# Unequal half blocks in a gated FFN after windowed attention: five pairs of 512, 512, 512, 384, 384 tokens instead of four pairs of 464 and one of 448

## The chip, the cores and the metric

The kernel runs on one core of a Trainium2 chip. The metric is the device time of one execution in microseconds (us). Beside each time there is a profile of one execution: its span, from the first to the last instruction, and what each engine did. The engines are PE (TensorE; PEld is its weight load), DVE (VectorE), ACT (ScalarE), POOL (GpSimd) and SP (SyncE, which here issues all the DMAs).

## The reference

Causal attention with a window of 128 positions and a linear bias over 8 batches, 8 heads, 576 positions, 64 per head; its output, 4608 tokens of 512, goes through a gated FFN of width 1536:

```python
scores = q @ k.T / 8 - slope[h] * |i - j|, kept where 0 <= i - j < 128
x = (softmax(scores) @ v) -> [4608, 512]
gate = 1 / (1 + exp(-(x @ w_gate)))          # w_gate, w_val: [512, 1536]
out = (gate * (x @ w_val)) @ w_out           # w_out: [1536, 512]
```

Weights arrive as 8-byte floats and are decoded on the chip to 4-byte ones.

## The kernel before

Every product of the FFN is done in three passes: both operands are split into a high and a low part (`parts`: a cast, then a subtraction), and high x high, high x low and low x high are summed in PSUM.

The work has three stages.

1. Attention, together with the first four of the twelve 128-wide chunks of the FFN's hidden layer h (`gates1`, line 514). It takes the tokens in nine tiles of 512; each output chunk of a tile is 12 matmuls of 512 columns (line 534).
2. The other eight chunks (`gates2`, line 586). The 4608 tokens are taken in five pairs of half blocks; `HALVES[t]` is the length N of a half block in pair t, and `EDGE` holds where each starts. Gate and value weights and the two half blocks are combined in a scheme of seven products for eight (Strassen's, in Winograd's form). `mix` makes the seven combinations of x for the pair (`combo`, the tiles cxA, cxB, cxC, each high and low part); `combine` made those of the weights once (w2s0 to w2s5, and w2s6 and w2s7 in the tile `w67`). A chunk is seven products of 6 matmuls of N columns each (line 616), 42 in all.
3. The output projection (`results`, line 683), in the same scheme and over the same five pairs. h has been written to DRAM (`hs`) by `spill` and is read back in four quadrants (half block h, half k of the hidden layer), each in three pieces of two chunks (`hquad`). For each of seven products and each third e the combination of h is split into one of `NHC` places (`hcombo`), and 12 matmuls of N columns follow (line 728), so a pair has 7 x 36 = 252 matmuls.

Stages 2 and 3 together have 5 x (8 x 42 + 252) = 2940 matmuls, 588 for each pair, whatever N is.

The ring (`ring`, line 200) is one tile of NRING places of N2 = max(HALVES) columns. Stage 1 uses its first 2048 columns as four places of 512. In stage 2 a chunk takes three places in turn (`scratch`): for a partial sum that is only read back, and for two results that are spilled to `hs`. In stage 3 a pair takes eight: two each for `a1`, `p5`, `u2` and `x`, which are stored to the output.

Where the quadrants of h lie: (0,0) in the place of xr, the input of `mix`; the other three in `hr`, in the place of `w67` (tag wA). The h pieces have nine places: seven are the combos of x, the two more (`hw`) lie in the weights' scratch (tag xW), which `combine` uses while it prepares the weights of the output projection (`wos`, in the places of w2s0 to w2s5).

The order of instructions on each engine is fixed beforehand by a planner (`Graph.order`): it lists every operation with an estimated cost, and each time starts the one that can start first. PE's order is thus fixed too: an operand that comes later than planned makes PE wait. `follow` says that a buffer's new contents must wait until its old ones were used. The planner's cost of a PE group is, for six matmuls,

```python
g.add("PE", 6 * (N / 2400 + 0.0133), six, ...
```

The last call of `gates2` takes the chunks in the order 6, 7, 0, 1, 2, 3, 4, 5, since `hr` waits for w2s6 and w2s7, and `wos{c}` for w2s{c}.

Of the kernel before, what the change touches and what calls it, by code (L numbers as in the profile page):

```python
# [8 lines left out]
F32 = mybir.dt.float32  # L9
I32 = mybir.dt.int32  # L10
F32R = mybir.dt.float32r
# [4 lines left out]
P = 128  # L16
# [7 lines left out]
NFC = DFF // P  # L24
NB = 512
NTB = NT // NB
FC1 = 4
GRP = 2
HALVES = (464, 464, 464, 464, 448)
N2, NT2 = max(HALVES), len(HALVES)  # L30
EDGE = [2 * sum(HALVES[:b // 2]) + b % 2 * HALVES[b // 2] for b in range(2 * NT2)] + [NT]
HC = NFC // 6
NRING, NRING1, NHC = 10, 4, 9
HEAD = 8
RUN = 4
NPB, NST, NPT, NBOTH = 8, 10, 3, 3
# [11 lines left out]
NRAW = 2  # L48
# [110 lines left out]
def attention_gated_ffn(ctx: ExitStack, tc: tile.TileContext, qd, kd, vd, wg, wv, wo, out):  # L159
# [6 lines left out]
    moe = ctx.enter_context(tc.tile_pool(name="moe", bufs=1))  # L166
# [6 lines left out]
    def T(pool, name, shape, dtype, tag=None):  # L173
        if name not in made:
            made[name] = pool.tile(shape, dtype, tag=tag or name, name=name)
        return made[name]
# [50 lines left out]
    xs = [dram.tile([KC, P, S], F32, name=f"xs{b}") for b in range(B)]  # L227
    hs = [[dram.tile([NFC // 2, P, HALVES[b // 2]], F32, name=f"hs{k}_{b}") for b in range(2 * NT2)] for k in range(2)]
    wod = [dram.tile([P, DM], F32, name=f"wod{f}") for f in range(NFC)]
# [20 lines left out]

    w1 = lambda kind, part_: T(moe, "w1", [P, 2, 2, FC1, DM], F32R, tag="wA")[:, "gv".index(kind), part_]
    w67 = lambda: T(moe, "w67", [P, 2, 2, 7, 2 * P], F32R, tag="wA")
    hr = lambda: T(moe, "hr", [P, 3, NFC // 2, N2], F32, tag="wA")
    w2t = lambda i, part_: w67()[:, i - 6, part_] if i > 5 else T(pools["w2"], f"w2s{i}", [P, 2, 7, 2 * P], F32R, tag=f"W{i}")[:, part_]
    wot = lambda c, part_: T(pools["w2"], f"wos{c}", [P, 2, 7, 2 * P], F32R, tag=f"W{c}")[:, part_]
    x1 = lambda part_: T(moe, "x1", [P, 9 * DM], F32R, tag="xB")[:, part_ * KC * NB:(part_ + 1) * KC * NB].rearrange("p (c t) -> p c t", c=KC)
# [1 line left out]
    wraw = lambda s: work()[:, s * 2 * DM:(s + 1) * 2 * DM].rearrange("p (f t) -> p f t", t=2)  # L258
    wbits = lambda s: work()[:, (4 + s) * DM:(5 + s) * DM]
# [298 lines left out]
    ORDER = (0, 3, 4, 1, 5, 2, 6)  # L558
# [7 lines left out]
    def combo(k, part_):  # L566
        j, grp = [(j, n) for n, ks in (("xA", (0, 3, 4)), ("xB", (1, 5, 2)), ("xC", (6,))) for j, kk in enumerate(ks) if kk == k][0]
        return T(moe if grp == "xB" else pools["w2"], f"c{grp}", [P, 1 if grp == "xC" else 3, 2, 2, N2], F32R, tag=grp)[:, j, part_]
# [17 lines left out]
    def gates2(t, chunks, f0):  # L586
        F = FIRST + 1
        N, t0 = HALVES[t], EDGE[2 * t]
        xr = lambda: xrow()
# [83 lines left out]
        split(6, x(1, 1), xk[1, 1])  # L673

    hq0 = lambda: T(moe, "hq0", [P, NFC // 2, N2], F32, tag="xr")
    hquad = lambda h, k: hq0() if h == k == 0 else hr()[:, {(1, 0): 0, (1, 1): 1, (0, 1): 2}[h, k]]

    def hcombo(s, part_):
        if s < len(ORDER):
            return combo(ORDER[s], part_)  # L680
        return T(moe, "hw", [P, 2, 2, HC, N2], F32R, tag="xW")[:, s - len(ORDER), part_]

    def results(t):
        F, N, t0 = FIRST + 2, HALVES[t], EDGE[2 * t]
        third = [slice(e * HC, (e + 1) * HC) for e in range(3)]
# [8 lines left out]
        def split(k, e, val, reads):  # L694
            s = slots[k, e]
            parts(lambda: hcombo(s, 0)[:, :, 0:N], lambda: hcombo(s, 1)[:, :, 0:N], val, m, reads, ("hc", s, 0), ("hc", s, 1), F)
# [10 lines left out]
        def product(k, banks_, start):  # L707
            for e in range(3):
                v = lambda a, b, e=e: (lambda: hquad(a, b)[:, third[e], 0:N])
                q = lambda a, b: hk[a, b, e]  # L710
                if k == 3:
                    add(v(1, 0), v(1, 0), v(1, 1), ALU.add, q(1, 1), q(1, 0))
                elif k == 4:
                    add(v(1, 0), v(1, 0), v(0, 0), ALU.subtract, q(0, 0), q(1, 0))
                elif k == 5:
                    add(v(0, 1), v(0, 1), v(1, 0), ALU.subtract, q(1, 0), q(0, 1))
                    add(v(1, 0), v(1, 1), v(1, 0), ALU.subtract, q(1, 1), q(1, 0))
                a, b = {0: (0, 0), 3: (1, 0), 4: (1, 0), 1: (0, 1), 5: (1, 0), 2: (0, 1), 6: (1, 1)}[k]
                split(k, e, v(a, b), q(a, b))
                s = slots[k, e]  # L720
                for i in range(2):
                    if len(banks_) == i:
                        banks_.append(bank())

                    def six(i=i, e=e, s=s):
                        for c in range(HC):
                            for j, (xp, wp) in enumerate(((0, 0), (0, 1), (1, 0))):
                                nc.tensor.matmul(mm[banks_[i]][:, 0:N], wot(e * HC + c, wp)[:, k, i * P:(i + 1) * P], hcombo(s, xp)[:, c, 0:N],  # L728
                                                 start=(start and e == c == j == 0), stop=(e == 2 and c == HC - 1 and j == 2),
                                                 skip_group_check=True)  # L730
                    wa = 0 if k < 1 else 1
                    g.add("PE", 3 * HC * (N / 2400 + 0.0133), six,
                          [("hc", s, 0), ("hc", s, 1)] + [("wo", e * HC + c, p, wa) for c in range(HC) for p in range(2)],
                          [("mm", banks_[i])], 1.0e6)
# [74 lines left out]
    def follow(old, new):  # L809
        g.add("PY", 0.0, lambda: None, [], [*old, *new], FIRST)  # L810

    both_ = lambda *k: [(*k, p) for p in range(2)]
# [5 lines left out]
    w2k = lambda i: [("w2", i, p, a) for p in range(2) for a in (0, 2)]  # L818
# [17 lines left out]
        wsrc = [wo[f] for f in range(NFC)]  # L836
    for t in range(NT2 - 1):
        gates2(t, range(NW), FC1)
    gates2(NT2 - 1, (6, 7, 0, 1, 2, 3, 4, 5), FC1)
    follow(w2k(6) + w2k(7), [("hq", h, k, e) for h, k in ((1, 0), (1, 1), (0, 1)) for e in range(3)])  # L840
    follow([("xr", k, (h, e)) for k in range(2) for h in range(2) for e in range(2)], [("hq", 0, 0, e) for e in range(3)])
    follow([("wraw", s) for s in range(NRAW)], [("tt", 1)])
    for c in range(NFC // 2):
        follow(w2k(c), wok(c))
        combine(wsrc[c], wsrc[c + NFC // 2], 1, lambda p, c=c: wot(c, p), ("wo", c), [("wod", c), ("wod", c + NFC // 2)], FIRST + 1.5, c % 2)
    for s0, c in enumerate(ORDER):
        follow(both_("xc", c), both_("hc", s0))
    follow([("wraw", s) for s in range(NRAW)] + [("wbits", s) for s in range(2)] + [("tt", j) for j in range(2)], both_("hc", 7) + both_("hc", 8))
    for t in range(NT2):
        results(t)  # L850
    g.play()
# [51 lines left out]
```

## Time and profile before

| | |
|---|---|
| median of three runs | 1022.43 us (1020.39 to 1022.81) |
| profiled execution, its time | 1021.79 us |
| its span | 1020.1 us |
| PE busy | 1002.2 us (98%), 6450 matmuls |
| PEld busy | 848.3 us (83%) |
| DVE, ACT, POOL busy | 786.0, 499.1, 116.9 us |
| DMA | 158.48 MB, mean 155 GB/s |
| mean granted PE clock | 0.996 |
| first matmul of stage 2 | at 400.6 us |
| last matmul's end | at 1015.6 us |

A row of the timeline or the windows counts instructions in flight in its stretch. The mean duration of a matmul is its latency; matmuls are pipelined, so what a matmul takes of the time is the distance from its start to the next one's start, which is shorter.

### The profile page before, as it was taken

Reading aid. Unit: us, or ns where it says so; the run is one execution under the profiler, and the core shown is the slowest. Engines: PE = TensorE matmul, PEld = TensorE weight load, DVE = VectorE, ACT = ScalarE, POOL = GpSimd, SP = SyncE. Lnnn points to the kernel's source line nnn. Section 1 sums busy time; section 2 is a strip of 40 time slices with the busy share of each in tenths; the row PEclk is TensorE's granted clock in tenths of the full one; section 3 lists DMA queues with packets and bytes.
Section 4 is the critical chain, followed back from the end, with each engine's and each line's share of the span. In section 5 each row is a group of like instructions: output and inputs, shape, how many; then the busy total and the mean of one; then the engine's idle time right before and its main releaser. Section 6 shows DMA issues by size and latency. Waiting matters only on the chain.

```text
span 1020.1 us, 18313 instructions
## 1 busy us (share of the span) xinstructions
PE 1002.2 (98%) x6450; PEld 848.3 (83%) x6450; DVE 786.0 (77%) x2011; ACT 499.1 (49%) x1309; POOL 116.9 (11%) x214
## 2 busy tenths in 40 slices
PE   9899899999999999999999999999999999999998
PEld 7667677777777788888888888889988888888897
DVE  7999888888868897869447356365898888898881
ACT  6998777777864334445334334343464423222220
POOL 2333343333320000100000000000100000000000
PEclk9999899999999999999999999999999999999999
DMA  8776765656435554774313113116435363534201
GB/s 288 262 235 205 228 213 196 231 162 232 145 116 186 168 184 157 241 240 156 130 47 122 57 56 129 57 57 245 144 106 199 114 186 114 170 128 137 100 3 70
DMA packets 88316, 158.48 MB, mean 155 GB/s; under 512 B 11680, under 2 KB 63776, under 8 KB 88224
## 3 DMA queue, kind: packets, MB, share of 16 engines
q1 hardware_dynamic: 88224, 157.32, 46.1%
q8 instruction: 50, 0.82, 0.3%
q14 instruction: 42, 0.34, 0.1%
HBM read 106.95 MB, written 50.33 MB: 154 GB/s over the span
## 4 chain that ended last, share of the span: by engine, by line
PE 75%; DVE 13%; ACT 7%; issue 2%; DMA 2%; SPq 0%; DVEq 0%; ACTq 0%
PE mm L616 34%; PE mm L728 26%; PE mm L534 11%; ACT pb L391 4%; DVE mm L376 3%; DVE pb L388 2%; DVE pb L412 1%; PE mm L416 1%; PE mm L477 1%; ACT pb L411 1%; PE mm L353 1%; DVE st L406 1%; DVE x L189 1%; DMA work<-in_moe_w_gate_dram 1%; PE mm L363 1%
## 5 line engine op out<-in xcount | busy, mean ns | idle before, releaser
L534 PE MATMUL mm<-x,w 128*128 128x512 f32 x864 | 222.5, 402 | 3.7 <-DVE x L189 2.6
L534 PEld LDWEIGHTS mm<-x,w 128*128 128x128 f32 x864 | 155.2, 188 | 44.2 <-issue 7.6
L391 ACT ACTIVATE pb<-pb,st 128x128 f32<-128x128 f32 x288 | 112.8, 395 | 39.8 <-DVE st L388 39.4
L427 POOL TENSOR_SCALAR_AFFINE_SELECT pt<-both 128x384 f32<-128x384 f32 x192 | 100.4, 546 | 193.0 <-ACT both L180 163.6
L616 PE MATMUL mm<-cxB,w2s 128*128 128x464 f32 (+1 forms) x540 | 119.5, 372 | 0.1
L616 PE MATMUL mm<-cxA,w2s 128*128 128x464 f32 (+1 forms) x540 | 118.5, 370 | 0.0
L728 PE MATMUL mm<-cxA,wos 128*128 128x464 f32 (+1 forms) x540 | 114.4, 370 | 0.0
L616 PEld LDWEIGHTS mm<-cxB,w2s 128*128 128x128 f32 x540 | 101.5, 188 | 12.2 <-ACT ring L180 0.5
L623 DVE TENSOR_TENSOR mm<-mm,ring 128x464 f32<-128x464 f32 (+1 forms) x80 | 51.3, 643 | 77.9 <-PE mm L616 77.8
L728 PEld LDWEIGHTS mm<-cxA,wos 128*128 128x128 f32 x540 | 101.3, 188 | 11.1
L616 PEld LDWEIGHTS mm<-cxA,w2s 128*128 128x128 f32 x540 | 101.3, 188 | 11.0
L627 ACT ACTIVATE sg<-mm 128x464 f32<-128x464 f32 (+1 forms) x80 | 44.4, 556 | 120.7 <-PE mm L616 76.0
L180 ACT COPY ring<-mm 128x464 f32<-128x464 f32 (+1 forms) x119 | 64.6, 544 | 75.3 <-PE mm L616 74.9
L728 PE MATMUL mm<-cxB,wos 128*128 128x464 f32 (+1 forms) x360 | 77.2, 372 | 0.0
L728 PEld LDWEIGHTS mm<-cxB,wos 128*128 128x128 f32 x360 | 67.7, 188 | 7.8
L388 DVE CUSTOM_DVE_ANT_0 pb<-mm,relm 128x128 f32<-128x128 f32 x288 | 68.4, 284 | 1.7
L188 POOL TENSOR_TENSOR work<-work 128x256 f32<-128x256 f32 x9 | 11.7, 1304 | 431.7 <-DMA work<-wod 296.9
L416 PE MATMUL mm<-ident,pb 128*128 128x128 f32 x288 | 52.9, 289 | 7.5 <-ACT both L180 4.1
L740 ACT ACTIVATE ring<-mm 128x464 f32<-128x464 f32 (+1 forms) x40 | 22.2, 555 | 75.9 <-PE mm L728 75.9
L376 DVE COPY_PREDICATED mm<-swap,mm 64x128 f32<-64x128 int32 x216 | 55.2, 294 | 4.8 <-PE mm L363 1.2
L411 ACT ACTIVATE pb<-pb,st 128x128 f32<-128x128 f32 x157 | 54.1, 395 | 8.7 <-DVE st L408 8.5
L416 PEld LDWEIGHTS mm<-ident,pb 128*128 128x128 f32 x288 | 33.1, 142 | 27.9 <-ACT both L180 10.3
(107 smaller groups left out, 1620.5 us busy)
## 6 DMA issues: line engine op xcount, KB each, us to landing
kr<-in_k_dram SPq DMA_DIRECT2D x31, 576.0 KB, 4.7
hr<-hs SPq DMA_DIRECT2D x36, 464.0 KB, 4.6
hs<-ring SPq DMA_DIRECT2D x68, 232.0 KB, 2.0
qr<-in_q_dram SPq DMA_DIRECT2D x31, 320.0 KB, 5.1
vr<-in_v_dram SPq DMA_DIRECT2D x32, 288.0 KB, 3.7
xs<-xt SPq DMA_DIRECT2D x32, 288.0 KB, 3.1
out_dram<-ring SPq DMA_DIRECT2D x32, 232.0 KB, 2.5
work<-in_moe_w_gate_dram SPq DMA_DIRECT2D x12, 512.0 KB, 4.3
```

The source lines that it names most:

```text
L180: g.add("ACT", act_cost(n, psum), lambda: nc.scalar.copy(out(), src()), reads, writes, want, release=release, ways=[("DVE", dve_cost(n, ps ...
L376: g.add("DVE", dve_cost(2 * D, psum=True), lambda b=b, col=col, to=to, of=of: nc.vector.copy_predicated(sp[b][col, :, to:to + D], swap[col ...
L388: g.add("DVE", 0.21, lambda: nc.vector.tensor_tensor_reduce(pb()[:, e], sp[j // 2][:, j % 2, first:first + P], relm[u.p][:, w], op0=ALU.ad ...
L391: g.add("ACT", 0.39, lambda: nc.scalar.activation(pb()[:, e], pb()[:, e], AF.Exp, bias=st()[:, e:e + 1], scale=-1.0, accum_out=st()[:, 3 + ...
L411: g.add("ACT", 0.3, lambda args=args: nc.scalar.mul(*args()), [(kst, 6)], [(kpb, e)], want, ways=[("DVE", 0.16, True, lambda args=args: nc ...
L416: nc.tensor.transpose(tp[:, e], pb()[:, e], ident)
L427: nc.gpsimd.affine_select(pt(u)[:, f0:f0 + 2 * n - 1:2, :], both(), [[0, n], step], cmp, 0.0, base=0, channel_multiplier=mult)
L534: nc.tensor.matmul(mm[s], w1(kind, wi)[:, i, c * P:(c + 1) * P], x1(x)[:, c, :], start=(k == 0 and c == 0), stop=(k == 2 and c == KC - 1))
L616: nc.tensor.matmul(mm[b][:, 0:N], w2t(i, wp)[:, wk, c * P:(c + 1) * P], combo(k, xp)[:, c, 0:N], start=(start and c == 0 and j == 0), stop ...
L623: g.add("DVE", dve_cost(N, psum=True), lambda: nc.vector.tensor_tensor(o(), bk(b)(), a(), op=ALU.add), [("mm", b), *reads] if okeys else r ...
L627: g.add("ACT", act_cost(N, psum=True), lambda: nc.scalar.activation(sg[h](), bk(b)(), AF.Tanh, scale=0.5), [("mm", b)], [("sg", h)], F)
L728: nc.tensor.matmul(mm[banks_[i]][:, 0:N], wot(e * HC + c, wp)[:, k, i * P:(i + 1) * P], hcombo(s, xp)[:, c, 0:N], start=(start and e == c ...
```

## The change

The total number of tokens stays 4608 and the number of matmuls stays the same; three pairs have half blocks of 512 tokens, two of 384. N2 grows from 464 to 512, and with it each buffer that holds a half block. To make room, the ring has six places instead of ten, h pieces seven instead of nine, and `hr` two quadrants instead of three; the quadrant (0,1) of h goes into the weights' scratch, where the two extra h pieces were, and so waits until the last `combine` has been done. In the last call of `gates2` the order of chunks becomes 0, 6, 1, 7, 2, 3, 4, 5.

```diff
-HALVES = (464, 464, 464, 464, 448)
+HALVES = (512, 512, 512, 384, 384)
...
-NRING, NRING1, NHC = 10, 4, 9
+NRING, NRING1, NHC = 6, 4, 7
...
-    hr = lambda: T(moe, "hr", [P, 3, NFC // 2, N2], F32, tag="wA")
+    hr = lambda: T(moe, "hr", [P, 2, NFC // 2, N2], F32, tag="wA")
+    hw = lambda: T(moe, "hw", [P, NFC // 2, N2], F32, tag="xW")
...
-    hquad = lambda h, k: hq0() if h == k == 0 else hr()[:, {(1, 0): 0, (1, 1): 1, (0, 1): 2}[h, k]]
+    hquad = lambda h, k: hr()[:, k] if h else hw() if k else hq0()
 
     def hcombo(s, part_):
-        if s < len(ORDER):
-            return combo(ORDER[s], part_)
-        return T(moe, "hw", [P, 2, 2, HC, N2], F32R, tag="xW")[:, s - len(ORDER), part_]
+        return combo(ORDER[s], part_)
...
-    gates2(NT2 - 1, (6, 7, 0, 1, 2, 3, 4, 5), FC1)
-    follow(w2k(6) + w2k(7), [("hq", h, k, e) for h, k in ((1, 0), (1, 1), (0, 1)) for e in range(3)])
-    follow([("xr", k, (h, e)) for k in range(2) for h in range(2) for e in range(2)], [("hq", 0, 0, e) for e in range(3)])
+    gates2(NT2 - 1, (0, 6, 1, 7, 2, 3, 4, 5), FC1)
+    hq = lambda *hk: [("hq", h, k, e) for h, k in hk for e in range(3)]
+    follow(w2k(6) + w2k(7), hq((1, 0), (1, 1)))
+    follow([("xr", k, (h, e)) for k in range(2) for h in range(2) for e in range(2)], hq((0, 0)))
...
-    follow([("wraw", s) for s in range(NRAW)] + [("wbits", s) for s in range(2)] + [("tt", j) for j in range(2)], both_("hc", 7) + both_("hc", 8))
+    follow([("wraw", s) for s in range(NRAW)] + [("wbits", s) for s in range(2)] + [("tt", j) for j in range(2)], hq((0, 1)))
```

## The prediction

> **What bounds the kernel now.** I read the page's head first, then the chain of work that ended last, then the windows and the timeline of PE in the last two stages.
>
> ```profile
> span 1020.1 us, 18313 instructions
> PE 1002.2 (98%) x6450; PEld 848.3 (83%) x6450; DVE 786.0 (77%) x2011; ACT 499.1 (49%) x1309; POOL 116.9 (11%) x214
> PEclk9999899999999999999999999999999999999999
> ...
> 336.60 64.21 PE mm L534 x282
> 400.81 341.33 PE mm L616 x1632
> 749.50 1.49 PE mm L616 x6
> 751.00 2.52 PE mm L728 x12
> 753.52 1.22 PE mm L616 x6
> 754.74 260.84 PE mm L728 x1248
> ```
>
> From 336.60 us to the end the chain is PE alone, matmul behind matmul, at full granted clock. The windows of these stages:
>
> ```profile
> core 0: us, PE busy (x) PEld busy (x) DVE busy (x) ACT busy (x) POOL busy (x), PEclk, DMA share, GB/s
> 345.00:395.00 50.00, 50.00 (x223) 41.39 (x222) 41.85 (x71) 17.66 (x28) 0.00 (x0) 1.00 0.58 197
> 425.00:675.00 250.00, 250.00 (x1188) 222.71 (x1187) 143.87 (x216) 96.62 (x167) 3.10 (x3) 1.00 0.33 111
> 700.00:745.00 45.00, 45.00 (x225) 41.88 (x224) 35.03 (x56) 17.41 (x29) 5.40 (x5) 1.00 0.58 198
> 740.00:760.00 20.00, 19.89 (x97) 17.88 (x96) 19.34 (x27) 13.63 (x19) 1.95 (x2) 1.00 0.21 72
> 770.00:940.00 170.00, 170.00 (x808) 151.53 (x807) 146.58 (x158) 53.59 (x68) 0.00 (x0) 1.00 0.48 151
> 400.64:1015.56 614.92, 614.81 (x2941) 551.95 (x2939) 444.75 (x576) 225.09 (x347) 11.69 (x9) 1.00 0.38 125
> ```
>
> Stages 2 and 3 take 614.92 us and PE stands still in 0.11 us of them. So their time is the number of matmuls (2940, one more counted in flight) times the distance from one start to the next. A busy PE does not say what that distance is, so I take it from the timeline, from the starts of two neighbouring rows:
>
> ```profile
> 339.66 61.14 PE L534 MATMUL mm<-x,w 128*128 128x512 f32 x269
> 400.64 6.42 PE L616 MATMUL mm<-cxA,w2s 128*128 128x464 f32 x30
> 406.90 1.42 PE L616 MATMUL mm<-cxB,w2s 128*128 128x464 f32 x6
> ...
> 797.63 15.27 PE L728 MATMUL mm<-cxA,wos 128*128 128x464 f32 x72
> 812.74 7.80 PE L728 MATMUL mm<-cxB,wos 128*128 128x464 f32 x36
> 820.38 2.67 PE L728 MATMUL mm<-cxC,wos 128*128 128x464 f32 x12
> ...
> 986.36 7.44 PE L728 MATMUL mm<-cxA,wos 128*128 128x448 f32 x36
> 993.63 7.41 PE L728 MATMUL mm<-cxB,wos 128*128 128x448 f32 x36
> 1000.88 2.58 PE L728 MATMUL mm<-cxC,wos 128*128 128x448 f32 x12
> ```
>
> - 512 columns: (400.64 - 339.66) / 269 = **226.7 ns**, 0.4427 ns a column.
> - 464 columns: 15.11 / 72 = 209.9 and 7.64 / 36 = 212.2; over the window of 250 us, with the 0.37 us that a matmul is in flight, 250.37 / 1188 = **210.7 ns**, 0.454 a column.
> - 448 columns: 7.27 / 36 = 201.9 and 7.25 / 36 = 201.4; over the window from 700 us, 45.36 / 225 = **201.6 ns**, 0.450 a column.
>
> The planner's own cost, N/2400 + 0.0133 us, gives 226.6, 206.6 and 200.0. At 512 the chip does just that; at 464 it loses 4.1 ns a matmul, at 448 1.6 ns. The widths do not lie on one line: from 448 to 464 a column costs 0.57 ns, from 464 to 512 only 0.33. So 464 is a poor width. By these distances the stages are 2352 x 210.7 + 588 x 201.6 = 614.1 us, 0.8 under the window.
>
> **The change part by part.**
>
> The matmuls. 588 for each pair stay, so 3 x 588 = 1764 have 512 columns and 1176 have 384. For the former I take 226.7 ns: 399.9 us. It is the distance in a stretch of 269 matmuls with a weight load before each one, DVE at 84% (41.85 of 50 us) and DMA at 0.58, so other work does not disturb it. No row here has 384 columns, so I bound it. Low: proportional to the columns, from 512, 170.0 ns. High: the line through 464 and 512 carried on, 226.7 - 128 x 0.33 = 184 ns. The planner's form gives 173.3; with the loss of the width 448 added, 174.9. I take 174: like 512 it is a multiple of 128, and with N2 = 512 its rows lie at the same places as those of 512. 1176 x 174 = 204.6 us. Sum 604.5 against 614.9: **-10.4 us**. With 170 it is -15.1, with 184 it is +1.4.
>
> The other engines over a pair. DVE, ACT and DMA carry the same elements in as many instructions:
>
> ```profile
> 759.04 3.18 DVE L700 TENSOR_TENSOR hr<-hr,hq 128x928 f32<-128x928 f32 x3
> 762.15 1.11 DVE L189 TENSOR_TENSOR cxC<-hr,cxC 128x928 fp32r<-128x928 f32 x1
> hr<-hs SPq DMA_DIRECT2D x36, 464.0 KB, 4.6
> hs<-ring SPq DMA_DIRECT2D x68, 232.0 KB, 2.0
> ```
>
> One op on 928 elements takes 3.11 / 3 = 1.04 us of DVE; in proportion 1.14 at 1024 and 0.86 at 768. A pair of stage 3 has 21 subtractions for the splits and 12 adds: 38 us of DVE at 512, 28 us at 384, beside 252 matmuls that take 57 and 44 us. DVE has room, PE hides it: 0.
>
> Seven places for h pieces instead of nine. A third of a product is 12 matmuls, 2.72 us at 512. With seven places DVE can be six thirds ahead, 16 us, instead of eight. The heaviest product (line 715: two adds and a split in each third) needs 3 x 3 x 1.14 = 10.3 us of DVE against 8.2 us of PE, so the lead falls by 2.1 us there and is won back on the next product, which needs 3.4. The last split of a pair starts two thirds later, 5.4 us, and so does the read of the next pair's quadrant (1,1): the place is free about 12 thirds before that quadrant's piece is due, and the read takes 4.6 us. Cost 0; it would show from 10 us of lateness on.
>
> Six ring places instead of ten. In stage 2 a spilled place is needed again two chunks later, so its write to `hs` has one whole chunk, 42 x 0.2267 = 9.5 us at 512 and 7.3 at 384; it takes 2.0 us to land. What waits behind it would be ACT's copy, and after it PE's next product into that bank. In stage 3 the fourth pair of places takes those of a1, whose store was issued three products (over 18 us) before. Cost 0, at most what SP's queue is late beyond 5 us.
>
> The start of stage 2. The first combination that PE needs just in time is that of the fourth product:
>
> ```profile
> 404.85 1.11 DVE L189 TENSOR_TENSOR cxB<-xr,cxB 128x928 fp32r<-128x928 f32 x1
> ```
>
> It is ready at 405.96 and PE takes it at 406.90: 0.94 us to spare. With 512 the input's read (5.9 us for the 928 KB of `xr`, a tenth more) and eight DVE operations come some 1.3 us later, and PE's need 30 x 16 ns = 0.5 us later. 0.1 us is left: take 0.2, bounds 0 and 1. The other four changes of pair have the same balance; where PE was slower than planned at 464 it gave the others 4 ns a matmul (0.17 us a chunk) of slack, and that is gone: 0.3 in sum, bounds 0 and 2.
>
> The end of stage 2 into stage 3. From 740 to 760 us DVE is busy 19.34 of 20 us and PE misses 0.11, the only place where DVE is that full. The last pair's chunks now take PE 7.3 us instead of 8.5, so three chunks give 3.5 us less for the weights of the output projection; but these start two chunks earlier (chunk 0 first), DVE's ops of the chunk shrink by a seventh, and the first thirds of stage 3 last 2.72 us instead of 2.53. Quadrant (0,1) is read only after the last of these weights: DVE ends them at 759.04, 4.4 us after the last chunk, and product 1 needs it 3 x 36 x 0.2267 = 24.5 us after. The two quadrants in `hr` wait for chunks 6 and 7 until half of the pair, 29 us before its end, and are read in 5 us. I take 0.5, bounds 0 and 4.
>
> The first stage. Nothing in attention changes; 512-token spills meet the edges of the first three pairs, so there are fewer writes to `hs`, and the planner may order some things otherwise. Bounds -1.5 and +1.5, taken 0. The tail behind the last matmul has 64 columns less in two ACT operations and a store: 0.
>
> Sum: -10.4 + 0.2 + 0.3 + 0.5 = **-9.4 us**. The profiled execution took 1021.79 us, so 1012.4; the median of the three runs is 0.64 above it: **1013.0 us**.
>
> **The rivals.**
>
> 1. *The loss belongs to the stage, not to the width.* If each matmul of stages 2 and 3 loses 4.1 ns against the planner's cost whatever N is, the sum is 614.9 again: columns and matmuls are the same in number. Time 1022.4. For it: short runs of 512 among attention's matmuls are slow too; this one is 2.77 / 12 = 231 ns, 4 above the long run.
>
> ```profile
> 298.94 2.77 PE mm L534 x12
> ```
>
> Against it: 448 columns in the same stage lose only 1.6. The Trainium skill, "TensorE: Matmul & The Clock Gate", section "Back-to-back issue gap", has such a rule: columns over the clock plus a fixed 2.5 ns, from which this change would bring nothing either. The trace does not follow it: the cost above the columns changes between 464 and 448.
>
> 2. *Narrow matmuls meet the weight load* (the other side). Every matmul brings its own load:
>
> ```profile
> L534 PEld LDWEIGHTS mm<-x,w 128*128 128x128 f32 x864 | 155.2, 188 | 44.2 <-issue 7.6 <-DVE x L189 4.5 <-ACT sg L544 1.5
> L728 PEld LDWEIGHTS mm<-cxA,wos 128*128 128x128 f32 x540 | 101.3, 188 | 11.1
> ```
>
> It lasts 188 ns at any width. If a matmul can't follow the one before within a load and some 3 ns, 384 columns take 191: 1176 x 0.191 = 224.6, sum 624.5, +9.6 us: 1032. It decides from 182.8 ns on, where the sum is again 614.9. Against it: these 24 matmuls of 128 columns, each with its own load, follow at (24.62 - 21.84) / 24 = 116 ns, so loads do overlap.
>
> ```profile
> 21.84 2.84 PE L240 MATMUL mm<-ident 128*128 128x128 f32 x24
> 24.62 1.13 PE L353 MATMUL mm<-kr,qr 64*128 64x256 f32 x8
> ```
>
> 3. *The ring of six makes PE wait.* If spills land late behind SP's queue, each of the 40 chunks waits; from 0.24 us a chunk on the gain is eaten; at 0.4 us it is +16 - 9.4 = +6.6: 1029. For it: SP issues everything in one order and waits long in it.
>
> ```profile
> SPq L185 <- DVE ring L631: 206.0, 63, 8.6
> ```
>
> Against it: that is SP idle until DVE has a result, not a full queue; DMA is at 0.38 in these stages.
>
> 4. *A partial gain*: 384 at 178 to 180 ns, or waits of 4 to 6 us at the changes of stage: about 1018.
>
> **How the numbers follow.** My case 0.70, its own range 1008 to 1016 (384 columns at 170 to 175, waits 0 to 3). Partial gain 0.10. No change 0.09. Weight load 0.06, ring 0.05. The range 1008 to 1020 takes in my case and most of the partial one; what is left out is 0.2 for the rivals and a little of the tails. Runs of this kernel agree to about 0.3%, 3.1 us, so faster means below 1019.4: 0.70 + 0.09 of the partial case = 0.79; same 0.01 + 0.09 = 0.10; slower 0.11.
>
> **What would show it.** In the profile after: starts of L616 and L728 226.7 ns apart at 512, near 174 at 384; stage 2 begins at 400 to 401 us; stages 2 and 3 together 604 to 606 us; PE idle after 401 us below 2 us, with ACT ring L180 not waiting for DMA. Wrong I would be if 512 runs at 231 there, if 384 comes at 183 or above, or if PE stands still at changes of pair or between 730 and 770 us.

## The result, and the profile after

| | before | after |
|---|---|---|
| median of four runs each | 1021.79 us (1020.39 to 1022.81) | 1009.47 us (1008.50 to 1009.58) |
| profiled execution | 1021.79 us, span 1020.1 | 1009.42 us, span 1007.6 |
| stages 2 and 3, first start to last end | 614.92 us | 604.78 us |
| first matmul of stage 2 | at 400.64 us | at 399.49 us |
| store behind the last result, wait of SP | 2.5 us | 1.4 us |

The ratio is 0.9878 (95% interval 0.9861 to 0.9895): 12.3 us faster, where 9.4 were forecast; the time forecast was 1013.0 us, in a range of 1008 to 1020. Of the 12.5 us between the two spans, 10.1 lie in stages 2 and 3, about 1.15 before them and 1.15 behind them.

The head of the page, after:

```profile
span 1007.6 us, 18317 instructions
PE 991.4 (98%) x6450; PEld 831.5 (83%) x6450; DVE 790.7 (78%) x2014; ACT 497.9 (49%) x1307; POOL 113.8 (11%) x213
```

The chain of work that ended last, from stage 2 on (start, us, engine, line):

```profile
399.65 297.56 PE mm L617 x1404
697.28 0.17 issue
697.45 0.95 DVE wos L181
698.40 1.01 DVE ring L632
699.41 0.48 DVE mm L624
699.89 0.47 DVE ring L624
700.40 44.01 PE mm L617 x252
744.41 1.39 PE mm L727 x6
745.80 1.04 PE mm L617 x6
746.84 257.44 PE mm L727 x1254
1004.31 0.49 ACT ring L739
```

PE is still the chain in these stages. The one excursion to DVE, at 697 us, looks like 3 us of waiting, but it isn't: a chain goes back over DVE's work as soon as a matmul was released by DVE, however short the wait. What PE lost there is in the windows (columns as before):

```profile
690.00:710.00 20.00, 19.92 (x115) 19.61 (x114) 15.10 (x26) 7.45 (x16) 1.39 (x1) 1.00 0.47 156
705.00:740.00 35.00, 35.00 (x204) 35.00 (x203) 28.38 (x47) 13.28 (x26) 0.74 (x1) 1.00 0.56 184
...
399.49:1004.27 604.78, 604.70 (x2941) 534.79 (x2939) 447.43 (x577) 225.68 (x347) 8.66 (x8) 1.00 0.38 127
```

0.08 us are lost near 700, which is all that PE loses in both stages (0.11 before). The distances, from the starts of neighbouring rows of PE's timeline:

```profile
399.49 8.32 PE L617 MATMUL mm<-cxA,w2s 128*128 128x512 f32 x36
407.65 2.88 PE L617 MATMUL mm<-cxB,w2s 128*128 128x512 f32 x12
...
802.48 8.32 PE L727 MATMUL mm<-cxA,wos 128*128 128x512 f32 x36
810.64 8.32 PE L727 MATMUL mm<-cxB,wos 128*128 128x512 f32 x36
...
989.55 6.40 PE L727 MATMUL mm<-cxA,wos 128*128 128x384 f32 x36
995.79 6.40 PE L727 MATMUL mm<-cxB,wos 128*128 128x384 f32 x36
```

512 columns: 8.16 / 36 = 226.7 ns, in stage 2 as in stage 3. 384 columns: 6.24 / 36 = 173.3 ns. 1764 x 226.7 + 1176 x 173.3 = 603.7 us of the 604.78. So the time went where the sum said. What the sum took as its reason, that 464 is a poor *width*, is what the experiments are about: the change alters the width, the row stride and the place of every operand at once.

### The profile page after: what moved, and what is told of

The parts are those of the page before. It is cut to its first block, busy times and chain, and to the rows that moved or that the text cites. A ratio compares the mean times of both kernels' runs of the same rounds, so it can differ in the third digit from the quotient of the medians.

```text
span 1007.6 us, 18317 instructions
## 1 busy us (share of the span) xinstructions
PE 991.4 (98%) x6450; PEld 831.5 (83%) x6450; DVE 790.7 (78%) x2014; ACT 497.9 (49%) x1307; POOL 113.8 (11%) x213
## 4 chain that ended last, share of the span: by engine, by line
PE 78%; DVE 12%; ACT 7%; issue 2%; DMA 1%; SPq 0%; POOL 0%; ACTq 0%; DVEq 0%; POOLq 0%
PE mm L617 34%; PE mm L727 26%; PE mm L535 12%; ACT pb L392 4%; DVE mm L377 3%; DVE pb L389 2%; PE mm L417 1%; PE mm L364 1%; DVE pb L413 1%; PE mm L478 1%; PE mm L354 1%; DVE x L189 1%; ACT pb L412 1%; DVE xt L490 1%; DVE st L407 1%
## 5 line engine op out<-in xcount | busy, mean ns | idle before, releaser
L617 PE MATMUL mm<-cxA,w2s 128*128 128x512 f32 (+1 forms) x540 | 117.4, 367 | 0.0
L617 PE MATMUL mm<-cxB,w2s 128*128 128x512 f32 (+1 forms) x540 | 117.1, 367 | 0.0
L727 PE MATMUL mm<-cxA,wos 128*128 128x512 f32 (+1 forms) x540 | 113.7, 367 | 0.0
L727 PE MATMUL mm<-cxB,wos 128*128 128x512 f32 (+1 forms) x540 | 113.5, 367 | 0.0
L624 DVE TENSOR_TENSOR mm<-mm,ring 128x512 f32<-128x512 f32 (+1 forms) x80 | 51.1, 642 | 79.3 <-PE mm L617 79.0
L727 PEld LDWEIGHTS mm<-cxB,wos 128*128 128x128 f32 x540 | 98.3, 188 | 12.6
L628 ACT ACTIVATE sg<-mm 128x512 f32<-128x512 f32 (+1 forms) x80 | 44.4, 555 | 118.7 <-PE mm L617 72.5
L180 ACT COPY ring<-mm 128x512 f32<-128x512 f32 (+1 forms) x119 | 64.6, 544 | 71.0 <-PE mm L617 70.4
L392 ACT ACTIVATION_READ_ACCUMULATOR pb<-pb,st 128x1 f32 x288 | 54.6, 190 | 0.0
L739 ACT ACTIVATE ring<-mm 128x512 f32<-128x512 f32 (+1 forms) x40 | 22.2, 556 | 64.4 <-PE mm L727 64.4
```

The source lines that it names most:

```text
L180: g.add("ACT", act_cost(n, psum), lambda: nc.scalar.copy(out(), src()), reads, writes, want, release=release, ways=[("DVE", dve_cost(n, ps ...
L392: g.add("ACT", 0.39, lambda: nc.scalar.activation(pb()[:, e], pb()[:, e], AF.Exp, bias=st()[:, e:e + 1], scale=-1.0, accum_out=st()[:, 3 + ...
L617: nc.tensor.matmul(mm[b][:, 0:N], w2t(i, wp)[:, wk, c * P:(c + 1) * P], combo(k, xp)[:, c, 0:N], start=(start and c == 0 and j == 0), stop ...
L624: g.add("DVE", dve_cost(N, psum=True), lambda: nc.vector.tensor_tensor(o(), bk(b)(), a(), op=ALU.add), [("mm", b), *reads] if okeys else r ...
L628: g.add("ACT", act_cost(N, psum=True), lambda: nc.scalar.activation(sg[h](), bk(b)(), AF.Tanh, scale=0.5), [("mm", b)], [("sg", h)], F)
```

## The experiments

The theory that the prediction leaves: a matmul loses time by its width alone, at 464 and 448, and the change wins it back by going to 512 and 384. Its rivals: the row stride or the place of the operands costs it; other engines or DMAs disturb PE in these stages; and, the other way, the smaller buffers cost waits that hide a larger gain.

Each edit is against the kernel after, unless it says "before". Ratios are to runs of the kernel before on the same chip.

**Buffers of the change, old widths.**

```diff
-HALVES = (512, 512, 512, 384, 384)
+HALVES = (464, 464, 464, 464, 448)
```

> The buffers and the order of the change alone: six ring places, seven h pieces, a quadrant of h in the weights' scratch, chunks 0, 6, 1, 7 first, but the half blocks of before (464, 464, 464, 464, 448) at a row stride of 464. Theory W (the gain is that of the widths: 464 loses 4.1 ns a matmul, 512 and 384 nothing): matmuls 210.7 and 201.7 ns apart, stages 2 and 3 614 to 616 us, time as before, 1020 to 1024. Theory A (the loss comes from where the rows lie, at a stride of 464 columns): the same, since the stride is the same. Rival B (the buffers or the order bring part of the gain): below 1018. If the 1.15 us that stage 2 starts earlier come from the fewer spills at the pairs' edges, it starts at 400.6 us here.

Measured: 1017.71 us (1017.32 to 1018.14), ratio 0.9960 (0.9945 to 0.9975): 4 us faster than before, with widths that are the same, and just below the bound of 1018 set for rival B. Its windows (PE alone: us, PE busy, granted clock, DMA share, GB/s; then all engines):

```profile
425.00:675.00 250.00, 249.95 (x1197) 1.00 0.33 112
400.17:1011.95 611.78, 611.71 (x2941) 551.60 (x2939) 446.51 (x574) 225.32 (x349) 10.80 (x9) 1.00 0.38 125
```

The window from 425 us now holds 1197 matmuls where before had 1188, with no less DMA and no idle time to win: 464 columns take about 209 ns, not 210.7. The smaller ring and the seven places cost nothing. But 3.1 of the 10.1 us (614.92 - 611.78) are there without any change of width, and the other 7.0 come with the widths and the row stride.

**The same with the row stride of 512.**

```diff
-N2, NT2 = max(HALVES), len(HALVES)
+N2, NT2 = 512, len(HALVES)
```

> As the kernel lay464, but all buffers with rows of 512 columns (N2 = 512), of which 464 or 448 are used. Theory W (width): 210.7 and 201.7 ns still, 1020 to 1024. Theory A (the places of the rows): 206.7 and 200.0 ns, stages 2 and 3 604 us, time 1009 to 1012.

Measured: 1018.16 us (1016.92 to 1019.22), ratio 0.9963 (0.9950 to 0.9975). 464 columns take 208.9 to 209.2 ns, 448 take 202.6. Neither theory had this: the row stride alone does not bring 464 to the 206.6 of the planner's form, and 464 is below the 210.7 of before. Stages 2 and 3 take 611.7 us. This kernel and the change differ in HALVES alone, at the same buffers and the same row stride, so the 6.9 us down to 604.78 are those of the widths.

**Five other widths inside the kernel.** One execution each, at HALVES = (512, 480, 448, 448, 416) and (496, 468, 456, 452, 432).

> The changed kernel with half blocks of 512, 480, 448, 448, 416, all at a stride of 512 columns. By the planner's cost 226.7, 213.3, 200.0, 200.0 and 186.7 ns, 604 us in stages 2 and 3. Theory W: 448 stays at 201.7, and 480 and 416 lose 1.5 to 4 ns each: 608 to 612 us in these stages, time 1013 to 1017. Theory A: all at the planner's cost, time about 1010.

> The changed kernel with half blocks of 496, 468, 456, 452, 432 at a stride of 512 columns; no multiple of 64 among them, 468, 456 and 452 no multiple of 16. By the planner's cost 220.0, 208.3, 203.3, 201.7 and 193.3 ns, 604 us. Theory W: most of them lose about 4 ns, stages 2 and 3 at 610 to 617 us, time 1015 to 1022; it shows which widths lose. Theory A: the planner's cost, about 1010.

Measured: 1017.3 and 1021.5 us, at the upper ends of theory W's ranges. The second has a row stride of 496, its longest half block, not the 512 that its expectation names. Distances: 512: 226.9, 480: 216.7, 448: 202.7, 416: 188.4 ns; then 496: 225.5, 468: 211.7, 456: 204.4 to 208.3, 452: 203.4, 432: 197.7. Over N/2400 + 13.3 ns they lose 0.2, 3.4, 2.7, 1.8 and 5.5, 3.4, 1.1 to 5.0, 1.8, 4.4. So the loss is no simple function of the width: at one row stride 496 and 432 columns lose 5.5 and 4.4, and 452 between them 1.8.

**The same matmuls with nothing beside them.** Behind the end of the kernel, 23 series of 72 matmuls, PE alone at work: 15 widths with the operands of stage 3, then 464 columns with rows or weights shifted, then one fixed pair of operands.

```diff
+    for n_ in (512, 496, 480, 464, 448, 432, 416, 400, 384, 352, 320, 288, 256, 192, 128):
+        for o_, w_, x_, a_, z_ in burst(n_):      # as in stage 3: wos x cxA, 12 groups of 6
+            nc.tensor.matmul(o_, w_, x_, start=a_, stop=z_, skip_group_check=True)
+    for xo_ in (16, 32, 48): ...                  # 464 columns, rows from column xo_ on
+    for wo2_ in (16, 64, 128): ...                # 464 columns, weights from column wo2_ on
+    for n_ in (464, 512): ...                     # one fixed pair of operands
```

> The changed kernel with 1656 more matmuls behind the last one of the kernel, whose results go nowhere: 72 each of 512, 496, 480, 464, 448, 432, 416, 400, 384, 352, 320, 288, 256, 192 and 128 columns, in the kernel's pattern of six into a bank; then 464 with its rows read from 16, 32, 48 columns further on, 464 with its weights from another place, and 464 and 512 with always the same rows and weights. DVE, ACT and DMA do nothing beside them. Its time is longer by these, some 300 us. Theory W (a property of the width on PE itself): 512 and 384 at 226.7 and 173.3 ns, 464 at 208.5 to 211, 496 about 225, also with PE alone. Rival C (contention): the other engines' access makes the loss, and here every width is at columns/2400 + 13.3 ns. If multiples of 128 are the good widths, 256 is at 120.0 and 320 loses some ns; if multiples of 64 beside them, 320 is at 146.7. If the loss depends on the place in memory, the shifted series differ by 1 to 3 ns.

Windows of PE, each from the first start of one series to that of the next, so 72 distances (512, 496, 480, 464, 448, 416, 384, 320, 256, 192, 128 columns):

```profile
1002.34:1018.70 16.36, 16.36 (x73) 1.00 0.07 24
1018.70:1034.54 15.84, 15.84 (x73) 1.00 0.00 1
1034.54:1050.14 15.60, 15.60 (x73) 1.00 0.00 0
1050.14:1065.26 15.12, 15.12 (x73) 1.00 0.00 1
1065.26:1079.86 14.60, 14.60 (x74) 1.00 0.00 1
...
1093.95:1107.39 13.44, 13.44 (x73) 1.00 0.01 1
...
1120.36:1132.84 12.48, 12.48 (x73) 1.00 0.00 1
...
1144.44:1154.99 10.55, 10.55 (x73) 1.00 0.01 2
...
1164.48:1173.11 8.63, 8.63 (x75) 1.00 0.01 2
1173.11:1181.13 8.02, 8.02 (x75) 1.00 0.01 2
1181.13:1189.14 8.01, 8.01 (x74) 1.00 0.00 0
```

With DMA at 0.00 and every other engine still, 464 columns take 15.12 / 72 = 210.0 ns, near the 210.85 that they take in stage 3 of the kernel before. So the loss does not need DVE, ACT or DMA beside it. Here 496, 416, 384, 320 and 256 columns cost the planner's form, 480 and 464 cost 3.4 ns more, 448 costs 2.8 more. From 496 to 480 columns a matmul gains 3.3 ns, from 416 to 400 (where the series has 180.0) 6.7. From 192 to 128 columns the distance falls no further, 8.0 / 72 = 111 ns. For 496 the expectation of about 225 missed: it took 225.5 in the kernel above and takes 220.0 here; 416 took 188.4 and takes 186.7.

The shifted series say what else matters. Behind each series' first group of six, 464 columns with the rows 16, 32, 48 columns (64, 128, 192 bytes) further take 210.0, 213.3, 213.3 ns; with the weights 16, 64, 128 columns (64, 256, 512 bytes) further 213.3, 210.1, 210.1; with one fixed pair of operands 210.1, and 512 columns 226.8. A matmul of one width has several prices, by where its operands lie.

**Does the same show in the kernel before?** I sorted the distances at 464 in its trace by the tiles that a matmul reads. Two pairs of neighbouring rows of its timeline:

```profile
599.17 3.93 PE L616 MATMUL mm<-cxB,w 128*128 128x464 f32 x18
602.94 1.43 PE L616 MATMUL mm<-cxC,w 128*128 128x464 f32 x6
604.21 3.98 PE L616 MATMUL mm<-cxA,w 128*128 128x464 f32 x18
608.03 3.93 PE L616 MATMUL mm<-cxB,w 128*128 128x464 f32 x18
```

cxB with `w67`: 3.77 / 18 = 209.4 ns; cxA with `w67`: 3.82 / 18 = 212.2. Over the whole trace, cxA and cxC with w2s or wos, and cxB with w67, take 208.7 to 209.8 ns; the crossed pairs (cxB with w2s or wos, cxA or cxC with w67, hw with wos) take 211.4 to 212.1. By the buffers' sizes the starts of the tiles of the first kind lie a multiple of 256 bytes apart, those of the second 128 bytes more. All ten pairs of tiles fall on the right side. (A row of 464 columns has 1856 bytes, so inside a tile the operands lie at several distances; each price is a mean over these.)

**Is it the distance between operands, or the place itself?** An unused tile of 16 or 32 columns at the front of the first pool moves everything by 64 or 128 bytes (edit of before; [P, 32] in the second):

```diff
+    const.tile([P, 16], F32, name="pad")
```

> The kernel before with an unused tile of 16 columns (64 bytes in each partition) put first, so that everything behind it lies 64 bytes further on; nothing else is changed. If the distance at 464 depends on the place in memory, it changes from 210.6 and 210.85 ns to something between 208.9 and 213.3, stages 2 and 3 by up to -4 or +6 us, and the time with them: 1017 to 1028. If the 3.2 us that the kernel lay464 gains in these stages come from its buffers or its order, nothing changes here: 1021 to 1022.

> The same with 32 columns, 128 bytes. Place: another distance at 464 than before or than with 16 columns, 1017 to 1028; else 1021 to 1022. In both the change's widths would not be touched by it, since 512 and 384 kept their distance in every kernel.

Measured: 1022.01 us, ratio 0.9999 (0.9989 to 1.0008), and 1022.22 us, ratio 1.0007 (0.9997 to 1.0017). 464 columns take 210.56 and 210.85 ns in the two stages, as in a second profile of before itself (one execution, 1021.97 us), 210.56 and 210.84.

> The kernel before once more, unchanged, for how much a profile differs from one execution to the next: start of stage 2 (400.6 us), distance at 464 (210.7 ns), time behind the last ACT operation's start (4.5 us). If the 1.15 us at the start of stage 2 and the 1.2 us at the end are of the kernel, they are the same here within 0.3 us; if they are chance, they scatter by 0.5 to 1.

In this second profile stage 2 begins at 400.86 us, 0.2 later than in the first; from the last matmul's end to the end of the span it has 4.4 us, the first 4.5.

The place itself does nothing. Then the distance between the operands was changed alone: 32 unused columns behind `hr` put the two kinds of tiles 128 bytes further apart (edit of before), and 16 series of 72 at the end price four widths at four distances of rows and weights.

```diff
-    hr = lambda: T(moe, "hr", [P, 3, NFC // 2, N2], F32, tag="wA")
+    hr = lambda: T(moe, "hr", [P, 3 * (NFC // 2) * N2 + 32], F32, tag="wA")[:, 0:3 * (NFC // 2) * N2].rearrange("p (h c n) -> p h c n", h=3, c=NFC // 2)
...
+    for n in (512, 384, 464, 448):    # 72 each with the weights 0, 16, 32, 48 columns further
```

> The kernel before with 32 unused columns (128 bytes) behind its buffer hr, so that the tiles of weights w2s and wos and of cxA and cxC lie 128 bytes further on against cxB, hw and w67; and behind its last matmul 1152 more whose results go nowhere, 72 each of 512, 384, 464 and 448 columns, each with weights 0, 16, 32 and 48 columns (0, 64, 128, 192 bytes) further on against the rows. Theory P (at a poor width the distance depends on where rows and weights lie to each other, modulo 256 bytes): in the kernel before, those pairs of tiles that lie 128 bytes off modulo 256 are at 211.4 to 212.1 ns, the others at 208.7 to 209.8; here all lie at 0, so 464 comes down to 208.8 to 210.0 everywhere, as in the kernel lay464, and stages 2 and 3 take 611 to 612 us instead of 614.9. If the 3.2 us of lay464 come from its buffers or its order, 464 stays at 210.6 and the stages at 614.9. In the series behind, 464 and 448 change by 1 to 4 ns with the place of the weights. If 512 and 384 are free of loss wherever the operands lie, they are at 226.7 and 173.3 in all four places; if they were only lucky in their place, they lose some ns in one or two of them. The time is longer by the series, some 240 us.

The window of PE over its stages 2 and 3:

```profile
400.68:1013.00 612.32, 611.98 (x2942) 1.00 0.38 125
```

Its timeline at the end, one row for each series (distances 0 and 64 bytes of 512, 384 and 464 columns):

```profile
1012.84 16.51 PE L860 MATMUL mm<-cxA,wos 128*128 128x512 f32 x72
1029.18 16.96 PE L862 MATMUL mm<-cxA,wos 128*128 128x512 f32 x72
...
1079.19 12.67 PE L868 MATMUL mm<-cxA,wos 128*128 128x384 f32 x72
1091.69 12.88 PE L870 MATMUL mm<-cxA,wos 128*128 128x384 f32 x72
...
1129.56 15.22 PE L876 MATMUL mm<-cxA,wos 128*128 128x464 f32 x72
1144.62 15.52 PE L878 MATMUL mm<-cxA,wos 128*128 128x464 f32 x72
```

Unused memory makes stages 2 and 3 2.6 us faster (612.32 against 614.92; the expectation had 611 to 612), though PE stands still for 0.34 us in them instead of 0.11: 464 columns take 208.9 in stage 2 and 210.0 in stage 3 with every pair of tiles, and the dear pairs are gone. These are also the prices of the first experiment, 208.9 and 210.0, so the distance accounts for nearly all of the 3.1 us that it left unexplained. The series, as distances in ns behind each series' first group of six, with the weights 0, 64, 128, 192 bytes further:

| columns | 0 | 64 | 128 | 192 |
|---|---|---|---|---|
| 512 | 226.7 | 233.4 | 232.3 | 228.9 |
| 384 | 173.3 | 176.7 | 176.0 | 173.3 |
| 464 | 208.9 | 213.3 | 213.3 | 210.0 |
| 448 | 206.7 | 202.3 | 204.0 | 200.0 |

Of the four distances, only 0 leaves 512 without loss; at the worst it costs 6.7 ns more, 11.8 us on 1764 matmuls, more than the gain in these stages. With N2 = 512 a row of 2048 bytes keeps the operands there. Why a distance costs what it costs stays open: 448 at distance 0 takes 206.7 here and 202.8 in the earlier series, so the distance at the operands' start isn't all of it.

**Is there a limit below 384, and a better split?**

```diff
-HALVES = (512, 512, 512, 384, 384)
+HALVES = (512, 512, 512, 512, 256)
```

> The changed kernel with half blocks of 512, 512, 512, 512, 256. Theory W: 256 too is without loss, 120.0 ns, and stages 2 and 3 have 2352 x 226.7 + 588 x 120.0 = 603.8 us of matmuls, as the changed kernel has. If weight loads of 188 ns bound narrow matmuls, 191 ns, 41.7 us more: about 1051. The last pair's chunks take PE 5.0 us, and DVE needs 1.7 us for them and some 4 for the weights of the projection beside it, 5.7: it is late by 0.7 us a chunk, so I expect waits of 2 to 8 us there: 1011 to 1018.

Measured: 1012.87 us (1012.33 to 1014.61), ratio 0.9919 (0.9905 to 0.9934), as expected. 256 columns take 120.0 ns, where a weight load shows 188: no limit yet. The sum of distances is that of the change, 4 x 588 x 226.7 + 588 x 120.0 = 603.8 us; the 3 us more come from the change of stage. The profiled execution is the slowest of the four, 1014.61 us. Its timeline (in brackets: the idle time before, and who ended it):

```profile
760.46 0.63 PE L727 MATMUL mm<-cxB,wos 128*128 128x512 f32 x2
763.12 3.72 PE L727 MATMUL mm<-cxB,wos 128*128 128x512 f32 x10 [2.02 <-DVE cxB L189]
```

Two of its windows:

```profile
758.00:763.00 5.00, 3.09 (x14) 2.22 (x12) 5.00 (x5) 4.13 (x5) 0.00 (x0) 1.00 0.33 115
763.00:768.00 5.00, 4.88 (x14) 3.91 (x15) 5.00 (x6) 2.78 (x4) 0.00 (x0) 0.66 0.90 284
```

A chunk of 256 columns is 42 x 0.120 = 5.0 us, too short for DVE's work beside it: DVE is at 5.00 of 5 us and PE waits 2.02. Behind that wait the granted clock is 0.66 in the next window, and seven matmuls start 427 ns apart instead of 227, with slower ones beside them: 1.7 us more. So this wait is paid nearly twice.

**The order of the last chunks.**

```diff
-    gates2(NT2 - 1, (0, 6, 1, 7, 2, 3, 4, 5), FC1)
+    gates2(NT2 - 1, (6, 7, 0, 1, 2, 3, 4, 5), FC1)
```

> The changed kernel with the chunks of the last pair in the old order 6, 7, 0, 1, 2, 3, 4, 5. If the new order is what keeps the shorter chunks of the last pair free of waits, PE idles 1 to 4 us between 690 and 765 us, time 1010.5 to 1014. If it does nothing, 1009 to 1010.

Measured: 1011.0 us (1010.15 to 1011.64), ratio 0.9900 (0.9884 to 0.9917), 1.5 us above the change by the medians, at the edge of what these runs resolve. As expected (1 to 4 us), its trace has a wait that the new order removes:

```profile
745.42 1.19 PE L727 MATMUL mm<-cxA,wos 128*128 128x512 f32 x4 [1.01 <-DVE cxA L189]
```

Behind this wait of 1.01 us the granted clock stays at 1.00:

```profile
745.40:750.40 5.00, 4.98 (x23) 4.30 (x24) 5.00 (x8) 2.68 (x4) 0.00 (x0) 1.00 0.14 51
```

**The long pairs last.** DVE is fullest in the last pair's chunks, so longer chunks there should help.

```diff
-HALVES = (512, 512, 512, 384, 384)
+HALVES = (512, 384, 384, 512, 512)
```

> The changed kernel with the pairs in another order, 512, 384, 384, 512, 512: the same matmuls, but the last pair's chunks take PE 9.5 us instead of 7.3, so DVE has time for the weights of the projection. If the short last pair is what costs the waits that are left between 690 and 770 us (0.4 us), they vanish; behind the last matmul it has 0.2 to 0.5 us more. 1008.5 to 1010.5, no difference to the changed kernel that counts.

In this order part of the output is wrong: the input of a longer pair is read over a part of the shorter pair's input that is still to be used; the matmuls are the same in number and size. Measured: 1015.27 us (1014.93 to 1016.20), ratio 0.9934 (0.9919 to 0.9949): a miss by some 5 us. The wait in its timeline, and the first matmuls of the next long pair:

```profile
546.47 1.65 PE L617 MATMUL mm<-cxB,w2s 128*128 128x384 f32 x4 [3.41 <-DVE cxB L189]
598.74 1.55 PE L617 MATMUL mm<-cxA,w2s 128*128 128x512 f32 x6
```

The step of its chain just before the wait's end, DVE's operation that ends it, and the window just after:

```profile
540.98 4.38 DMA xr<-xs
```

```profile
545.46 0.96 DVE L189 TENSOR_TENSOR cxB<-xr,cxB 128x768 fp32r<-128x768 f32 x1 [4.54 <-DMA xr<-xs]
```

```profile
546.50:552.00 5.50, 5.50 (x24) 5.50 (x25) 2.42 (x5) 1.83 (x4) 0.00 (x0) 0.72 0.75 226
```

The wait lies 52 us before the long pair begins, and DVE's operation has 768 columns, so it is a combination of the second short pair. It is held up by the read of the next, long pair's input into the same place (four transfers, as that pair's tokens need; a short pair's need three), the fault that makes the output wrong; at the change from short to long itself PE does not wait. PE waits 3.41, and again the clock falls (0.72 over the next 5.5 us). So this run does not show what the long pairs last would cost by themselves. None of the versions beats the change.

## Why the prediction was right, point by point

- *Matmuls, -10.4:* the way from distances to time holds; 512 at 226.7 was right to the digit, and 384, taken at 174 between 170 and 184, is 173.3. But that the sum came out was in part luck. It set 604.5, a bare sum of distances, against 614.9, the window of before, which is 0.8 over its own bare sum (614.1). Like with like it forecast -9.6; the bare sum went from 614.1 to 603.7, -10.4, since 384 was taken 0.7 ns too high, 0.8 us. The two errors cancelled.
- *Its reason, that 464 is a poor width:* half right. About 7.0 us are the widths', with operands where they lie in these kernels; about 3.1 us come without any change of width, nearly all from the operands' distance. The two prices that the prediction quoted at 464, 209.9 (cxA) and 212.2 (cxB), were this difference; it averaged them to 210.7 and went on. The clause "its rows lie at the same places as those of 512" was what made 174 safe: at 64 bytes' distance 384 takes 176.7.
- *Waits, +1.0 (0.2, 0.3, 0.5):* hardly any to be seen. PE is idle for 0.08 us in both stages. The window is 1.1 over the bare sum (604.78 - 603.7) and was 0.8 over it before, so 0.3 at most came. Ring, seven places and DVE's load cost 0, as taken; the buffers alone brought no wait at the old widths either.
- *Change of stage, 0.5 (0 to 4):* about 0 with the new order; with the old one 1.5 by the medians, so the order was a part of the gain that the sum did not list by itself.
- *First stage, 0 (-1.5 to 1.5):* -1.15, inside. It ends, and stage 2 begins, between 399.59 and 400.86 in five profiles with the old buffers, and between 397.64 and 401.50 in nine with the new ones. That is scatter over orders and executions; that fewer spills do it isn't shown.
- *Tail, 0:* mis-sized, -1.15. The last store's wait in SP's waits, before and after:

```profile
SPq L898 <- DMA out_dram<-ring: 2.5, 1, 2.5
```

```profile
SPq L898 <- DMA out_dram<-ring: 1.4, 1, 1.4
```

 It is 2.1 to 2.5 us in five profiles with the old buffers and 1.3 to 1.6 in nine with the new ones, at 448 columns in the last pair (1.5) as at 384. So the store's shorter wait isn't the 64 columns less, and comes with the buffers; the cause is open. The whole tail, from the last matmul's end to the end of the span, is 4.5 us before, 3.7 with the new buffers at the old widths and 3.4 with the change, so some 0.3 may be the columns'.
- *Rival 1, the loss belongs to the stage:* refuted, 512 and 384 lose nothing there. The rule of the Trainium skill ("TensorE: Matmul & The Clock Gate", "Back-to-back issue gap") of a fixed 2.5 ns over the columns, which that section gives for an isolated matmul, doesn't hold for the stream here: the runs have 13.3 at best, and up to 20 by width and distance.
- *Rival 2, the weight load:* refuted. In the window from 705 us PEld is busy 35.00 of 35 us at 173 ns a matmul and PE loses nothing: loads of 188 ns overlap. The least distance in the series of 72 is 111 ns.
- *Rival 3, the ring:* refuted. PE's idle time of 0.08 us leaves no room for 40 waits.
- *Rival 4, a partial gain:* did not come; 384 is at 173.3, and the waits are those above.

Why more than 9.4: about 0.7 in the stages, from waits that did not come, and 1.15 before and 1.15 behind them, which the sum took at 0. That the 1.15 before them, which is scatter, fell on the good side is luck.

## What to carry to other kernels

Where PE is the chain, take the distance between the starts of neighbouring matmuls, by width and by the tiles that they read: two prices at one width are a finding, not noise to average. Before choosing a width, time it with the operands where they will lie; here rows and weights a multiple of 256 bytes apart, with 512, 384 or 256 columns, cost nothing over the planner's form. If you split unequally, put the short pieces where the work that they must cover is short: the last pair of 256 columns brought a wait of 2.0 us and another 1.7 at a lower clock.

## What the runs showed of the hardware that was not expected

- The price of a matmul with its weight load depends on the distance between its two operands in memory: 226.7 to 233.4 ns at 512 columns, 208.9 to 213.3 at 464. Moving both together by 64 or 128 bytes changes nothing (ratios 0.9999 and 1.0007).
- It is not a smooth function of the width: in the series with PE alone 496 and 416 columns cost 13.3 ns over the columns, 480 and 464 between them 16.7. Nor is it one of the width alone: in the kernels with those widths 496 cost 18.8 over the columns and 416 15.1.
- Behind PE's waits of 2.02 and 3.41 us the granted clock was 0.66 over 5 us and 0.72 over 5.5, with matmuls of 512 columns 427 ns apart in the first and of 384 columns 320 ns apart in the second; behind one of 1.01 us it stayed at 1.00. That the waits are the cause is read from these three places, and no run tests it alone.
